# The last rows of an expert as a paired block, and smaller static shares

## The chip, the cores and the metric

The kernel runs on one core of a Trainium2 chip. The metric is the time of one execution on the device in microseconds (us), lower is better; the time given for a kernel is the median of its runs.

## What is computed

Three layers follow each other, in float32. Here is the reference, cut to the last one, which the change touches.

```python
def _moe2_ref(x, w_gate, w_output_gate, w1, w2):      # x: 1792 x 768, 8 experts, w1: 8 x 768 x 1024, w2: 8 x 1024 x 768
    logits = x @ w_gate
    e_idx = np.argmax(logits, axis=1)
    ...                                               # softmax: gate_w, one number per token
    eom = 1.0 / (1.0 + np.exp(-(x @ w_output_gate)))
    for e in range(E):
        mask = e_idx == e
        h = np.maximum(x[mask] @ w1[e], 0.0)
        ye = h @ w2[e]
        out[mask] = gate_w[mask, None] * eom[mask, e, None] * ye

def reference(**kwargs):
    attn_out = _attn_ref(...)                         # 4 batches, 12 heads, 448 tokens, 64 features
    x = attn_out.transpose(0, 2, 1, 3).reshape(1792, 768)
    x = _moe_ref(x=x, ...)                            # (sigmoid(x @ w_gate) * (x @ w_val)) @ w_out
    return _moe2_ref(x=x, ...)
```

Each token goes to one expert, the one of its largest logit.

## The kernel before

**Precision.** TensorE has a fast format, float32r, that keeps fewer bits of a number than float32. A float32 operand is therefore split into an upper part rounded to float32r and a lower part, the rest. A product of two split operands is taken in three passes: upper by upper, upper by lower, lower by upper. In the names `whi` and `wlo` are the parts of a weight piece (128 x 768), `gh` and `gl` those of the transposed tokens, `hh` and `hl` those of the hidden layer. In the trace both formats read as f32 matmuls.

**The stages.** Attention and the first dense layer come first and overlap; in them the rows of an expert's region in memory, `xg`, are filled with zeros in advance (`zero_rows`), and at their end a routing step gives every token a slot in its expert's region; scatters on GpSimd's queue put the tokens there. A planning step (`plan`) sorts the experts by count. The last part, `moe2`, then takes the experts in that order, j = 0 to 7, and for expert j a fixed number of rows, `CAPS[j]`, its static share. If an expert has more rows than its share, a branch at the end (`tc.If(some > 0)`, L1041 on) takes the remaining ones, 128 at a time, with the weights read again.

**One expert.** `gather(j)` reads its rows from `xg` by blocks of 128 (L918; the last block may be shorter) and, for a short block, copies of the row scales onto further partitions. `turn(j)` transposes them on TensorE (L936), ScalarE takes the upper part `gh` (L938) and VectorE the lower part `gl` (L939). `up2(j, f)`, for each of eight hidden blocks f, does 18 matmuls (six feature blocks by three passes, L957) with 128 x 128 of weights as the stationary operand and `CAPS[j]` columns of tokens as the moving one; ScalarE then takes relu and upper part (L963), VectorE the lower part (L964). `down2(j)` goes through the eight weight pieces of the second product; for each block of 128 rows the hidden block is the stationary operand and 384 columns of the weights the moving one, in two halves by three passes (L988), six matmuls. `finish(j)` multiplies by the row scale, on ScalarE (L1013) and in the last expert also VectorE (L1009), and scatters the rows to the output (L1016).

**The last rows.** A block of fewer than 128 rows has a path of its own (L980). The hidden rows stay whole in `hw`, float32 (L968), and so do the weights (`raw`); its 64 (or 32) rows take 64 (or 32) columns of the array, two (or four) such tiles side by side, each for a part of the 768 output columns:

```python
if rows < 128:
    c = DM * rows // 128
    for n in range(128 // rows):
        nc.tensor.matmul(
            ps[i, 0][n * rows:(n + 1) * rows, 0:c], lhsT=hw[f][:, 0:rows],
            rhs=w[2][:, LG + n * c:LG + (n + 1) * c], start=(f == 0), stop=(f == NF2 - 1))
```

**Weights and order.** An expert has 16 weight pieces of 384 KB. SyncE's queue loads them up to six ahead (L112), and they are split two ahead: ScalarE makes the upper part (L120), VectorE or GpSimd in turn the lower one (L122). The split parts stand in rings of four. The order of instructions on each engine is set by the framework's scheduler, which moves them within what the data allow; while `down2(j)` runs, the transposes of expert j + 1 are put between its matmuls, one feature block at a time, and parts of short blocks can come between the upward matmuls.

Of the kernel before, what the change touches and what calls it, by code (L numbers as in the profile page):

```python
# [8 lines left out]
F32 = mybir.dt.float32  # L9
# [10 lines left out]
CH = 112                       # queries or keys of a chunk; S is four of them  # L20
NPAIR = B * H // 2             # pairs of heads; a pair fills 128 features
# [5 lines left out]
LG = 2 * NE                    # logit columns beside the 768 of the output  # L27
WO = DM + LG
ROW = DM + 2                   # scale, token id, features
CAPS = [384, 320, 288, 256, 256, 256, 256, 192]   # rows that the static part takes, experts by count  # L30
CAPMAX = max(CAPS)
SQ_ACT = 1, 2                  # pairs whose squares ScalarE takes, and groups by their first pair whose roots VectorE
NEWTON_V = 0, 1
DIRECT = 0, 1, 2               # pairs whose rows of key scales come from the tensor engine alone
PARTS = 2                      # a piece of float64 comes in that many parts
# the last downward product of each half: blocks a to g, logits of its two token groups, their turn, the routing
FINAL = "a0b1ctrdefg", "01trabcdefg"
# what each slot of pair 0 prepares: splits, stats or key rows up to a pair, before all else where it is a capital
PREP = "s1 t2", "K1", "s2", "K2", "", "", "t4", ""
UNIT = 128.0                   # moe 1's outputs are kept divided by it: 1 / 256 comes with w_out, 2 with the gate  # L40
# [3 lines left out]
def attn_moe_moe_kernel(ctx, tc, qk, tokqk, tokv, g, wup, wout, wr, w1, w2, out):  # L44
# [26 lines left out]
    # ---------------------------------------------------------------- weights  # L71
    # a piece is 128 x 768, the 16 logit columns before it where it has them;
    # in: its float32 words are in SBUF, split: they lie there as two float32r parts
# [10 lines left out]
    def piece_in(n):  # L84
# [4 lines left out]
        if kind == "wide":  # L89
            for c in range(0, DM, DM // PARTS):  # L90
# [6 lines left out]
                # the upper word with its exponent in float32's place but for three bits, the lower one's upper three  # L97
# [67 lines left out]
    # -------------------------------------------------------------- attention  # L165
    # pools of which the first part of the attention has a second lot, in place of the moe's
# [54 lines left out]
    def halves(p):  # L221
        """the heads of a pair, by slices: the first pair's one by one"""
        return (slice(0, 1), slice(1, 2)) if p == 0 else (slice(0, 2),)
# [52 lines left out]
    def inv_root(grp):  # L276
        """(mean of squares + 1e-6) ** -0.5 by Newton's steps"""
# [20 lines left out]
    def row_bank():  # L298
        """a bank for what goes between the scores and the transposes, of its own as long as there is one"""
        if lots["ps_k"][2] is not None:  # L300
            return lots["ps_k"][2].tile([128, 4, CH], F32, tag="k", name="k")
        return tile_of("ps_t", [128, 4, CH], F32, "t")

    def krow(p):
# [4 lines left out]
        if p in DIRECT:  # L309
            # the first ones without the way through memory  # L310
# [159 lines left out]
    def prep(i):  # L470
        """what the first pairs need, in the slots of pair 0"""
# [25 lines left out]
    # -------------------------------------- logit columns: w_out times the router's weights  # L497
# [43 lines left out]
    # ------------------------------------------------------------------- moe 1  # L541
# [117 lines left out]
    # ----------------------------------------------------------------- routing  # L659
# [3 lines left out]
    def route(half):  # L663
# [23 lines left out]
        # ranks: tokens before this one of the same expert  # L687
# [9 lines left out]
        # the chosen expert's probability and output gate  # L697
# [4 lines left out]
        # slots  # L702
# [33 lines left out]
    def plan(tot):  # L736
        """Experts by falling count: tab = 8 experts, 8 counts past the static rows, 8 blocks of those, their sum."""
# [13 lines left out]
        # m[j, e] = (rank of e is j)  # L751
# [16 lines left out]
    # --------------------------------------------------------------- emission  # L768
# [15 lines left out]
    def setup2():  # L784
# [6 lines left out]
        # tri[t', t] = 1 where t' < t  # L791
# [39 lines left out]
    n = 0  # L831
# [34 lines left out]
    # second half: features come back and are split  # L866
# [15 lines left out]
def moe2(nc, tc, ctx, xg, w1, w2, out, tab, ident, add, ldpiece, drop, raw2, first):  # L882
# [31 lines left out]
    def gather(j):  # L914
        # float32's words as float32r, for transposes in one pass
        t = g_p.tile([128, 3, ROW], F32R, tag="g", name="g")
        for i, (r, n) in enumerate(blocks(j)):
            nc.sync.dma_start(out=t.bitcast(F32)[0:n, i, :], in_=xg[bass.ds(reg(j) * NT + r, n), :])  # L918
            for c in range(n, 128, n) if n < 128 else ():
                nc.sync.dma_start(out=t.bitcast(F32)[c:c + n, i, 0:1], in_=xg[bass.ds(reg(j) * NT + r, n), 0:1])  # L920
# [22 lines left out]
    def full(j):          # rows in blocks of 128  # L943
        return CAPS[j] // 128 * 128

    def up2(j, f):
# [13 lines left out]
        hh[f] = h_p.tile([128, CAPMAX], F32R, tag=f"hh{f}", name="hh")  # L960
        hl[f] = h_p.tile([128, CAPMAX], F32R, tag=f"hl{f}", name="hl")
        c0 = full(j)
        nc.scalar.activation(out=hh[f][:, 0:c0], in_=ps[:, 0:c0], func=ACTF.Relu)  # L963
        nc.vector.scalar_tensor_tensor(  # L964
            out=hl[f][:, 0:c0], in0=ps[:, 0:c0], scalar=0.0, in1=hh[f][:, 0:c0], op0=ALU.max, op1=ALU.subtract)
        if c0 < c:
            hw[f] = h_p.tile([128, 64], F32, tag=f"hw{f}", name="hw")
            nc.vector.tensor_scalar(out=hw[f][:, 0:c - c0], in0=ps[:, c0:c], scalar1=0.0, scalar2=None, op0=ALU.max)  # L968

    def down2(j):  # L970
        bl = blocks(j)
        ps = {(i, n): ps_d.tile([128, 512], F32, tag=f"d{i}{n}", name="d") for i in range(len(bl)) for n in range(2)}
        for f in range(NF2):
            w = ldpiece(("d", j, f))
            for i, (r, rows) in enumerate(bl):
                if rows < 128:
                    # few rows: column tiles of the array side by side, in float32
# [20 lines left out]
    def finish(j, ps):  # L998
        t = g_t.pop(j)
        for i, (r, rows) in enumerate(blocks(j)):  # L1000
            y = y_p.tile([128, DM], F32, tag="y", name="y")
            parts = 128 // rows if rows < 128 else 2
            c = DM // parts
            for n in range(parts):
                o, p = (i, n), 0
                if rows < 128:
                    o, p = (i, 0), n * rows
                if j == NE - 1 and n % 2:
                    nc.vector.tensor_scalar(  # L1009
                        out=y[0:rows, n * c:(n + 1) * c], in0=ps[o][p:p + rows, 0:c],  # L1010
                        scalar1=t.bitcast(F32)[p:p + rows, i, 0:1], scalar2=None, op0=ALU.mult)
# [152 lines left out]
```

## Time and profile before

| what | value |
|---|---|
| median of 3 runs | 1309.38 us |
| lowest and highest run | 1302.68 and 1311.21 us |
| profiled execution: its span, first to last instruction | 1302.4 us |
| TensorE's granted clock, mean over the span | 0.971 of full speed |

The profile is of one execution. The page gives its span and no other time of it, and it does not say which of the three runs it was, if any. A matmul's duration in the trace reaches past the start of the next one, since they are pipelined; what a stream of them costs is the time from one start to the next. Times within the profile are counted from the start of the span. The expert part begins at about 959 us.

### The profile page before, as it was taken

Reading aid. Unit: us, or ns where it says so; the run is one execution under the profiler, and the core shown is the slowest. Engines: PE = TensorE matmul, PEld = TensorE weight load, DVE = VectorE, ACT = ScalarE, POOL = GpSimd, SP = SyncE. Lnnn points to the kernel's source line nnn. Section 1 sums busy time; section 2 is a strip of 40 time slices with the busy share of each in tenths; the row PEclk is TensorE's granted clock in tenths of the full one; section 3 lists DMA queues with packets and bytes.
Section 4 is the critical chain, followed back from the end, with each engine's and each line's share of the span. In section 5 each row is a group of like instructions: output and inputs, shape, how many; then the busy total and the mean of one; then the engine's idle time right before and its main releaser. Section 6 shows DMA issues by size and latency. Waiting matters only on the chain.

```text
span 1302.4 us, 19952 instructions
## 1 busy us (share of the span) xinstructions
PE 1202.5 (92%) x7121; PEld 1041.0 (80%) x7121; DVE 737.0 (57%) x1688; ACT 593.4 (46%) x1173; POOL 387.0 (30%) x323
## 2 busy tenths in 40 slices
PE   4888889899899998998989999999969999999996
PEld 3656657678778887777879999999969888999994
DVE  7988987877678684855673143443443223333331
ACT  4666775556454553535332322212123344555552
POOL 3555655323142220411041000000032334444442
PEclk9897899999999999999999999999979999999999
DMA  9567557655436376595334111111074435665660
GB/s 218 141 160 181 160 148 216 180 162 167 123 125 196 107 218 181 148 237 145 123 130 155 54 49 61 50 56 42 1 278 165 168 103 183 251 223 209 208 218 19
DMA packets 79198, 194.04 MB, mean 149 GB/s; under 512 B 10543, under 2 KB 29487, under 8 KB 79088
## 3 DMA queue, kind: packets, MB, share of 16 engines
q1 hardware_dynamic: 76560, 181.64, 46.9%
q0 software_dynamic: 2528, 11.03, 2.2%
q8 instruction: 58, 0.95, 0.3%
q14 instruction: 52, 0.43, 0.1%
HBM read 154.97 MB, written 38.93 MB: 149 GB/s over the span
## 4 chain that ended last, share of the span: by engine, by line
PE 51%; DMA 3%; DVE 2%; issue 1%; SPq 1%; POOL 0%; ACT 0%; POOLq 0%; DVEq 0%
PE m L551 15%; PE d L988 11%; PE m L574 9%; PE u L957 8%; PE d L957 3%; DMA w<-in_wup_dram 2%; PE d L980 1%; PE a L430 1%; PE u L936 1%; DMA xg<-zrow 0%; DMA rs<-rsd 0%; DMA g<-xg 0%; PE t L409 0%; SPq L900 0%; PE m L593 0%
## 5 line engine op out<-in xcount | busy, mean ns | idle before, releaser
L120 ACT ACTIVATE whi<-raw 128x768 fp32r<-128x768 f32 (+1 forms) x200 | 167.0, 845 | 288.0 <-PE m L574 56.7
L122 POOL TENSOR_TENSOR wlo<-raw,whi 128x768 fp32r<-128x768 f32 (+1 forms) x100 | 190.8, 1913 | 312.8 <-ACT whi L120 289.1
L551 PE MATMUL m<-xh,whi 128*128 128x448 f32 x576 | 214.1, 372 | 6.6 <-DVE tanh L563 5.8
L122 DVE TENSOR_TENSOR wlo<-raw,whi 128x768 fp32r<-128x768 f32 (+1 forms) x100 | 101.3, 1017 | 205.9 <-ACT whi L120 197.6
L551 PE MATMUL m<-xl,whi 128*128 128x448 f32 x576 | 212.3, 369 | 0.0
L551 PE MATMUL m<-xh,wlo 128*128 128x448 f32 x576 | 210.5, 366 | 0.0
L381 ACT ACTIVATE e<-e,m,sy 112x448 f32<-112x448 f32 x192 | 144.9, 756 | 91.5 <-DVE m L378 90.8
L374 DVE CUSTOM_DVE_ANT_0 e<-s,rb 112x448 f32<-112x448 f32 x192 | 115.8, 612 | 19.4 <-PE s L363 11.5
L409 PE MATMUL t<-ident,e 112*112 112x112 f32 x768 | 112.4, 274 | 15.2 <-DVE et L415 5.3
L551 PEld LDWEIGHTS m<-xh,whi 128*128 128x128 f32 x576 | 109.2, 189 | 18.1 <-DVE tanh L563 6.5
L409 PEld LDWEIGHTS t<-ident,e 112*112 112x112 f32 x768 | 89.1, 140 | 43.1 <-issue 10.8
L574 PE MATMUL m<-whi,hhi 128*128 128x392 f32 (+1 forms) x336 | 115.5, 349 | 4.7 <-DVE acc L580 4.7
L551 PEld LDWEIGHTS m<-xl,whi 128*128 128x128 f32 x576 | 109.1, 189 | 9.6 <-issue 1.7
L574 PE MATMUL m<-wlo,hhi 128*128 128x392 f32 (+1 forms) x336 | 115.2, 343 | 1.3 <-POOL wlo L122 1.3
L551 PEld LDWEIGHTS m<-xh,wlo 128*128 128x128 f32 x576 | 109.0, 189 | 8.8
L430 PE MATMUL a<-et,v 112*64 112x224 f32 x768 | 110.9, 386 | 4.5 <-DVE xr L436 3.5
L362 PE MATMUL s<-K,Q 128*112 128x448 f32 x192 | 86.8, 452 | 30.5 <-DVE m L374 19.5
L574 PE MATMUL m<-whi,hlo 128*128 128x392 f32 (+1 forms) x336 | 114.2, 340 | 0.0
L335 POOL TENSOR_TENSOR Q<-qk,Q 64x896 fp32r<-64x896 f32 (+1 forms) x25 | 54.2, 2168 | 186.6 <-DVE Q L334 75.6
L417 ACT ACTIVATE et<-t 112x448 f32<-112x448 f32 x168 | 86.7, 531 | 29.2 <-PE t L409 28.9
L580 DVE TENSOR_TENSOR acc<-m,acc 128x392 f32<-128x392 f32 (+1 forms) x140 | 77.2, 559 | 33.6 <-PE m L574 32.4
L729 POOL DMA_INDIRECT xg<-acc,slot x14 | 14.4, 1029 | 272.5 <-DVE slot L706 268.6
(203 smaller groups left out, 2435.5 us busy)
## 6 DMA issues: line engine op xcount, KB each, us to landing
raw<-in_w_dram SPq DMA_DIRECT2D x128, 384.0 KB
qk<-in_qk_dram SPq DMA_DIRECT2D x46, 448.0 KB
w<-in_wup_dram SPq DMA_DIRECT2D x48, 384.0 KB
tok<-in_tokqk_dram SPq DMA_DIRECT2D x23, 448.0 KB
wf<-raw SPq DMA_DIRECT2D x24, 384.0 KB
w<-in_wout_dram SPq DMA_DIRECT2D x24, 384.0 KB
raw<-wf SPq DMA_DIRECT2D x24, 384.0 KB
rb<-rkd SPq DMA_DIRECT2D x21, 392.0 KB
```

Source lines behind the costliest of these rows:

```text
L120: nc.scalar.activation(out=hi[:, c:], in_=t[:, c:], func=ACTF.Copy)
L122: eng.tensor_tensor(out=lo[:, c:], in0=t[:, c:], in1=hi[:, c:], op=ALU.subtract)
L362: nc.tensor.matmul(ps, lhsT=lhs, rhs=K1_t[p][:, h, :], start=True, stop=False)
L374: nc.vector.tensor_tensor_reduce(out=e, in0=ps, in1=rb_t[p][:, h, :], scale=1.0, scalar=-3.0e38, op0=ALU.mult, op1=ALU.max, accum_out=m[:, ...
L381: nc.scalar.activation(out=e, in_=e, func=ACTF.Exp, scale=r_t[p][:, i:i + 1], bias=m[:, 1:2], accum_out=sum_t[p][:, i:i + 1])
L409: nc.tensor.transpose(ps[0:CH, kc, :], e[:, kc * CH:(kc + 1) * CH], ident[0:CH, 0:CH])
L417: nc.scalar.activation(out=dst, in_=ps[0:CH], func=ACTF.Copy)
L430: nc.tensor.matmul(ps[64 * h:64 * h + 64, hf * 2 * CH:(hf + 1) * 2 * CH], lhsT=v_t[p][:, h, kc, :], rhs=ets[h][:, kc, :], start=(kc == 0), ...
L551: nc.tensor.matmul(ps[:, 0:S], lhsT=a, rhs=x, start=(n == 0), stop=(n == 3 * KD - 1))
L574: nc.tensor.matmul(ps[:, 0:c1 - c0], lhsT=l, rhs=r, start=(i == 0), stop=(i == 5))
L957: nc.tensor.matmul(ps[:, 0:c], lhsT=a, rhs=x[:, k, 0:c], start=(n == 0), stop=(n == 3 * KD - 1))
L988: nc.tensor.matmul(ps[i, n][0:rows, 0:384], lhsT=l, rhs=s[:, c0:c0 + 384], start=(f == 0 and q == 0), stop=(f == NF2 - 1 and q == 2))
```

## The change

Two things are changed.

A last block of exactly 64 rows (`PAIRED`) is no longer computed in float32. Its upper parts and its lower parts are laid side by side in `hh`, 64 + 64 columns, as one stationary operand of 128 columns. Two passes, one with the upper and one with the lower part of the weights, then give the products of the upper rows on partitions 0 to 63 and of the lower rows on 64 to 127; `finish` adds the two halves: ScalarE scales the lower half into `y`, VectorE scales the upper half and adds. Such a block takes four matmuls a weight piece. A block of 32 rows keeps the old path, and blocks of over 64 rows take the ordinary path, where a block of 112 or 96 rows is now possible.

The static shares are smaller in four places: 384 to 320 (expert 0), 256 to 240, 224 and 192 (experts 4, 5 and 6). Experts 0, 1, 6 and 7 now end with a block of 64, expert 2 with one of 32. The rest of the difference is comments left out and line numbers moved by them; the first layers are the same.

```diff
-CAPS = [384, 320, 288, 256, 256, 256, 256, 192]   # rows that the static part takes, experts by count
+CAPS = [320, 320, 288, 256, 240, 224, 192, 192]
+PAIRED = 64
...
     def gather(j):
-            for c in range(n, 128, n) if n < 128 else ():
+            for c in range(n, 2 * n if n == PAIRED else 128, n) if n <= PAIRED else ():
...
-    def full(j):          # rows in blocks of 128
-        return CAPS[j] // 128 * 128
+    def full(j):
+        return sum(n for _, n in blocks(j) if n > PAIRED)
...
     def up2(j, f):
-        hh[f] = h_p.tile([128, CAPMAX], F32R, tag=f"hh{f}", name="hh")
+        hh[f] = h_p.tile([128, CAPMAX + PAIRED], F32R, tag=f"hh{f}", name="hh")
...
-        nc.scalar.activation(out=hh[f][:, 0:c0], in_=ps[:, 0:c0], func=ACTF.Relu)
+        c1 = c if c - c0 == PAIRED else c0
+        nc.scalar.activation(out=hh[f][:, 0:c1], in_=ps[:, 0:c1], func=ACTF.Relu)
...
-        if c0 < c:
-            hw[f] = h_p.tile([128, 64], F32, tag=f"hw{f}", name="hw")
+        if c0 < c1:
+            nc.vector.scalar_tensor_tensor(
+                out=hh[f][:, c1:c1 + PAIRED], in0=ps[:, c0:c1], scalar=0.0, in1=hh[f][:, c0:c1], op0=ALU.max,
+                op1=ALU.subtract)
+        elif c0 < c:
+            hw[f] = h_p.tile([128, PAIRED], F32, tag=f"hw{f}", name="hw")
...
     def down2(j):
-                if rows < 128:
+                if rows == PAIRED:
+                    for n in range(2):
+                        c0 = LG + n * 384
+                        for q in range(2):
+                            nc.tensor.matmul(
+                                ps[i, n][:, 0:384], lhsT=hh[f][:, r:r + 2 * rows], rhs=w[q][:, c0:c0 + 384],
+                                start=(f == 0 and q == 0), stop=(f == NF2 - 1 and q == 1))
+                    continue
+                if rows < PAIRED:
...
     def finish(j, ps):
-            parts = 128 // rows if rows < 128 else 2
+            parts = 128 // rows if rows < PAIRED else 2
             c = DM // parts
+            scale = t.bitcast(F32)[:, i, 0:1]
             for n in range(parts):
+                dst = y[0:rows, n * c:(n + 1) * c]
+                if rows == PAIRED:
+                    nc.scalar.activation(
+                        out=dst, in_=ps[i, n][rows:2 * rows, 0:c], func=ACTF.Copy, scale=scale[rows:2 * rows])
+                    nc.vector.scalar_tensor_tensor(
+                        out=dst, in0=ps[i, n][0:rows, 0:c], scalar=scale[0:rows], in1=dst, op0=ALU.mult, op1=ALU.add)
+                    continue
```

On TensorE, in expert 7's downward product, before: `hw` is the float32 block of 64 rows, with 64 of the array's columns.

```order
L988 MATMUL d<-whi,hh 128x384
L988 MATMUL d<-wlo,hh 128x384
L988 MATMUL d<-whi,hl 128x384
L980 MATMUL d<-raw,hw 64x384 x2
L988 MATMUL d<-whi,hh 128x384
L988 MATMUL d<-wlo,hh 128x384
L988 MATMUL d<-whi,hl 128x384
```

The same place after (L1003 is the ordinary block, L987 the paired one):

```order
L1003 MATMUL d<-whi,hh 128x384
L1003 MATMUL d<-wlo,hh 128x384
L1003 MATMUL d<-whi,hl 128x384
L987 MATMUL d<-whi,hh 128x384
L987 MATMUL d<-wlo,hh 128x384
L987 MATMUL d<-whi,hh 128x384
L987 MATMUL d<-wlo,hh 128x384
L1003 MATMUL d<-whi,hh 128x384
```

Two float32 matmuls on 64 columns have given way to four of the ordinary shape.

On TensorE, in the downward product of expert 5, where the transposes of expert 6 stand (`identr` marks a transpose, its shape ends with the rows turned), before:

```order
L936 MATMUL u<-identr,g 128x128 x2
L988 MATMUL d<-whi,hh 128x384
L988 MATMUL d<-wlo,hh 128x384
L988 MATMUL d<-whi,hl 128x384
L988 MATMUL d<-whi,hh 128x384
L988 MATMUL d<-wlo,hh 128x384
L988 MATMUL d<-whi,hl 128x384
```

The same place after; the 96 columns are the block of expert 5 with 96 rows:

```order
L1003 MATMUL d<-wlo,hh 128x384
L1003 MATMUL d<-whi,hl 128x384
L937 MATMUL u<-identr,g 128x128
L937 MATMUL u<-identr,g 128x64
L1003 MATMUL d<-whi,hh 96x384
L1003 MATMUL d<-wlo,hh 96x384
L1003 MATMUL d<-whi,hl 96x384
```

The second transpose of each feature block has 64 rows now instead of 128, and expert 5's second block has 96 columns as its stationary operand.

On VectorE, between expert 0 and expert 1, before (`gl` is the lower part of expert 1's transposed tokens, `hl` and `hw` belong to expert 1's first hidden block):

```order
L939 TENSOR_TENSOR gl<-u,gh 128x320 x2
L122 TENSOR_TENSOR wlo<-raw,whi 128x768
L939 TENSOR_TENSOR gl<-u,gh 128x320
L122 TENSOR_TENSOR wlo<-raw,whi 128x768
L964 SCALAR_TENSOR_TENSOR hl<-u,hh 128x256
L968 TENSOR_SCALAR hw<-u 128x64
```

The same place after (`y` are output rows of expert 0):

```order
L123 TENSOR_TENSOR wlo<-raw,whi 128x768
L940 TENSOR_TENSOR gl<-u,gh 128x320
L1025 SCALAR_TENSOR_TENSOR y<-d,g,y 64x384 x2
L123 TENSOR_TENSOR wlo<-raw,whi 128x768
L966 SCALAR_TENSOR_TENSOR hl<-u,hh 128x256
L969 SCALAR_TENSOR_TENSOR hh<-u,hh 128x64
```

The two additions into `y` stand ahead of a weight split and of the first hidden block; before, that split follows `gl` at once.

## Rows read from the trace of the kernel before

**Rows 1.** The page, busy time: us, share, instructions.

```profile
PE 1202.5 (92%) x7121; PEld 1041.0 (80%) x7121; DVE 737.0 (57%) x1688; ACT 593.4 (46%) x1173; POOL 387.0 (30%) x323
```

**Rows 2.** Windows, experts 0, 4, 6, 7, tail: us; busy (count) PE PEld DVE ACT POOL; clock; DMA; GB/s.

```profile
966.00:1022.00 56.00, 55.94 (x307) 54.55 (x307) 20.01 (x29) 23.83 (x42) 18.01 (x10) 0.95 0.51 173
...
1151.00:1186.00 35.00, 35.00 (x254) 34.79 (x254) 13.07 (x23) 19.21 (x35) 16.81 (x11) 1.00 0.63 226
...
1221.00:1257.00 36.00, 36.00 (x252) 34.66 (x251) 12.59 (x22) 18.73 (x35) 16.66 (x10) 1.00 0.66 225
1257.00:1292.00 35.00, 34.50 (x227) 26.20 (x225) 10.20 (x24) 14.09 (x25) 14.78 (x9) 1.00 0.24 81
1292.00:1303.00 11.00, 0.00 (x0) 0.00 (x0) 0.78 (x2) 0.23 (x1) 1.90 (x2) 0.70 0.15 51
```

**Rows 3.** Waits of TensorE's weight loads, 1116 to 1292: us, times, longest.

```profile
PEld d L988 <- POOL wlo L122: 0.6, 1, 0.6
```

**Rows 4.** Waits, 960 to 1303, ScalarE's split.

```profile
ACT whi L120 <- PE u L957: 48.2, 31, 5.2
```

**Rows 5.** The chain: start, us, what; upward 384, 320, 256, 192 columns, downward.

```profile
990.76 6.24 PE u L957 x36
...
1022.50 2.50 PE u L957 x17
...
1155.27 2.12 PE u L957 x18
...
1261.47 2.01 PE u L957 x18
```

```profile
1133.01 4.20 PE d L988 x24
```

**Rows 6.** The chain, first pieces of expert 7's downward product.

```profile
1273.54 1.07 PE d L988 x6
1274.61 0.80 PE d L980 x4
1275.40 1.24 PE d L988 x6
```

**Rows 7.** Timeline of TensorE at two turns, 128 + 64 rows and 128 + 128.

```profile
1242.13 0.40 PE L936 MATMUL u<-identr,g 128*128 128x128 f32 x2
...
1242.75 0.33 PE L988 MATMUL d<-wlo,hh 128*128 128x384 f32 x1
...
1207.08 0.29 PE L936 MATMUL u<-identr,g 128*128 128x128 f32 x2
...
1207.45 0.34 PE L988 MATMUL d<-wlo,hh 128*128 128x384 f32 x1
```

**Rows 8.** Timeline, the last transposes of expert 0.

```profile
965.22 1.01 PE L936 MATMUL d<-identr,g 128*128 128x128 f32 x6 [1.17 <-DMA g<-xg]
```

**Rows 9.** Windows, the first upward matmuls.

```profile
966.00:971.00 5.00, 4.94 (x16) 4.45 (x16) 4.24 (x7) 4.34 (x9) 1.98 (x2) 0.50 1.03 412
```

**Rows 10.** The chain at the end.

```profile
1290.61 0.56 PE d L988 x2
...
1292.27 0.63 DVE y L1009
...
1292.93 0.90 POOL out_dram L1016
...
1294.23 0.91 POOL out_dram L1016
```

**Rows 11.** Timelines, VectorE's split and TensorE's third upward group of expert 1.

```profile
1025.90 1.65 DVE L122 TENSOR_TENSOR wlo<-raw,whi 128x768 fp32r<-128x768 f32 x1 [4.77 <-ACT whi L120]
```

```profile
1028.16 0.38 PE L957 MATMUL u<-gh,whi 128*128 128x320 f32 x1 [0.40 <-DVE hw L968]
```

More of the change, by code (lines that the diff above doesn't have):

```diff
@@ L1001, in finish @@
             y = y_p.tile([128, DM], F32, tag="y", name="y")
-            parts = 128 // rows if rows < 128 else 2
+            parts = 128 // rows if rows < PAIRED else 2
             c = DM // parts
+            scale = t.bitcast(F32)[:, i, 0:1]
             for n in range(parts):
+                dst = y[0:rows, n * c:(n + 1) * c]
[5 more added lines that the diff above has]
+                    continue
                 o, p = (i, n), 0
-                if rows < 128:
+                if rows < PAIRED:
                     o, p = (i, 0), n * rows
@@ L1009, in finish @@
                     nc.vector.tensor_scalar(
-                        out=y[0:rows, n * c:(n + 1) * c], in0=ps[o][p:p + rows, 0:c],
-                        scalar1=t.bitcast(F32)[p:p + rows, i, 0:1], scalar2=None, op0=ALU.mult)
+                        out=dst, in0=ps[o][p:p + rows, 0:c], scalar1=scale[p:p + rows], scalar2=None, op0=ALU.mult)
                     continue
                 nc.scalar.activation(
-                    out=y[0:rows, n * c:(n + 1) * c], in_=ps[o][p:p + rows, 0:c], func=ACTF.Copy,
-                    scale=t.bitcast(F32)[p:p + rows, i, 0:1])
+                    out=dst, in_=ps[o][p:p + rows, 0:c], func=ACTF.Copy, scale=scale[p:p + rows])
             s = nc.gpsimd.indirect_dma_start(
```

## The prediction

> **What bounds the kernel now.** I read first the page's busy times and then a table of windows, one for each expert of the last part. TensorE is busy for 92% of the span [rows 1], and in the expert part for all of it: 35.00 of 35 us in expert 4, 36.00 of 36 in expert 6, while ScalarE, GpSimd and VectorE stand at 19, 17 and 13 us [rows 2]. The waits say the same from both sides. In the 176 us of experts 3 to 7 the weight loads of TensorE waited for a GpSimd split once, 0.6 us [rows 3]; ScalarE, which splits the weights, waited 48 us for TensorE to release them [rows 4]. So each matmul that goes from this part is worth its spacing, the time from its start to the next one's. The chain of waits gives that spacing, as time over count: going up, 6.24/36 = 0.173 us with 384 columns, 2.50/17 = 0.147 with 320, 2.12/18 = 0.118 with 256 and 2.01/18 = 0.112 with 192; going down 4.20/24 = 0.175 [rows 5].
>
> **The change part by part** (experts 0 to 7 in order of size; the routing of the reference on its inputs gives them 264, 262, 255, 254, 216, 211, 174 and 156 rows).
>
> *Expert 0, 384 to 320.* Upward 144 matmuls: 144 x (0.173 - 0.147) = 3.8 us. Downward the third block of 128 (six matmuls a piece) becomes a paired block of 64 (four), over eight pieces 16 fewer: 16 x 0.175 = 2.8. Together -6.6. Its first 5 us run at a granted clock of 0.50, the lower level, after the gather's idle time [rows 9]; that stays.
>
> *Experts 1 and 7, the last 64 rows.* Before, they go in full float32 with 64 columns of the array a time. Each such run takes 0.80 us, and the six ordinary matmuls between two runs take 1.24 instead of 6 x 0.175 = 1.05 [rows 6], so entering and leaving costs 0.19; a run is 1.0 us. Expert 7's downward stage lasts from 1273.54 [rows 6] to 1290.61 + 0.56 = 1291.17 [rows 10]: 17.6 us. Afterwards it holds 48 + 32 = 80 matmuls of one kind: 80 x 0.175 = 14.0, -3.6. Expert 1 has nine such runs in the order of before, 9.0 us, against 32 x 0.175 = 5.6: -3.4.
>
> The Trainium skill, TensorEngine Tiling (Array Packing), Key Properties, says that changing the tiling mode drains TensorE, and its table promises up to twofold speed for column tiles of 64. The trace agrees with the first by the 0.19 us; of the second it shows little, as the packed run of 0.80 is longer than the four full-width matmuls (0.70) that replace it.
>
> *Expert 6, 256 to 192.* Its second block turns into a paired one, 16 matmuls fewer: -2.8.
>
> *Narrower moving operands in experts 4, 5, 6 (240, 224, 192).* Below 256 columns the spacing hardly falls: 0.118 at 256 and 0.112 at 192 are the two ends for 240 and 224, so 144 matmuls save between 0 and 0.9 us each. From 384 columns down to 256 each 64 fewer bring about 0.027, the next 64 only 0.006, so I read 0.112 as a floor; 240 columns, 144 fewer than 384, would come to 0.173 - 144/64 x 0.027 = 0.112 and just reach it. 3 x 0.9 = -2.7.
>
> The Trainium skill, TensorE: Matmul & The Clock Gate, Back-to-back issue gap, puts the gap at columns/2.4 GHz + 2.5 ns, for 192 columns 82.5 ns. The trace does not agree (0.112); by that rule the three would save an estimated 6.7 us.
>
> *A transpose of 64 rows for expert 6.* It moves into expert 5's downward stage. A turn with 128 + 64 rows lasts from 1242.13 to 1242.75, one with 128 + 128 from 1207.08 to 1207.45 [rows 7]: 0.25 us more, six times: +1.5. The turns of 112 and 96 rows (experts 4 and 5) appear nowhere; their ends are 0 and +1.5 each, and I take 0, as they lie nearer to 128 than to 64.
>
> *Start.* The last transposes wait 1.17 us for the third gather [rows 8], which brings half the rows now, but another small DMA is queued behind it and six 64-row transposes follow: between -1.0 and +0.5, taken -0.5.
>
> *A new wait on VectorE.* The paired block is finished in two steps: ScalarE scales the lower half into y, then VectorE adds the upper half (a VectorE piece of y takes 0.63 us [rows 10]). VectorE stands in order: behind the two additions are the next expert's weight split and the release of its first upward bank. At that place before, a split of 1.65 us at 1025.90 already delays the release, and TensorE's third upward group begins only at 1028.16, with 0.40 us idle [rows 11]. Two additions cost some 1.3 us, but begin while VectorE was idle anyway. At the ends of experts 0, 1 and 6 I put 0 to 1 us each, +1.0 together. Elsewhere the added 64-column pieces on VectorE replace ones of the same size, or lie in its idle time (13 of 35 us busy [rows 2]); the smaller zero fill runs beside attention: 0.
>
> *Tail.* Before, the y pieces end with a VectorE one at 1292.27 + 0.63, then two scatters start at 1292.93 and 1294.23 [rows 10]. Now the last block needs two ScalarE and two VectorE steps in series with the first block's. The second scatter has 1.3 us of cover behind the first; the chain is some 1.2 longer: 0 to +1.2, taken +0.6.
>
> Sum: -6.6 - 3.6 - 3.4 - 2.8 - 2.7 + 1.5 - 0.5 + 1.0 + 0.6 = -16.5 us. Against the profiled execution's span of 1302.4 this is 1285.9. The median of the three runs is 7.0 above that span and the lowest run 0.3, so I set the difference against the median: 1309.4 - 16.5 = 1292.9, in round numbers 1293, -1.3%.
>
> **The rivals.** *The array changes its mode for 112 and 96 rows too.* For it speaks the 64-row turn [rows 7], against it only that these lie nearer to 128. It costs two sets of turns (+3.0) and, if the stationary operands of 112 and 96 columns drain it as well, 16 blocks x 0.19 = +3.0: 1299.
>
> *The weight split becomes the bound.* With TensorE some 2 to 4 us shorter in experts 4 to 7, ScalarE, GpSimd or the transfers would set the pace, and the terms of experts 4 to 7 (3.6 + 2.8 + 2.7 = 9.1) would be lost: 1302. Against it: expert 6 would take 36 - 2.8 - 0.9 = 32 us with ScalarE at 19 of it; expert 7's transfers have nearly ended when its downward stage begins, 81 GB/s in that window against 226 [rows 2].
>
> *The spacing goes on falling with the columns.* From 384 to 256 it falls by 0.055 for 128 columns, and at that slope 192 columns would give 0.090 and the three shares 144 x (0.007 + 0.014 + 0.028) = 7.0 instead of 2.7 us: 1289. Against it stands the row with 192 columns at 0.112 [rows 5]. The Trainium skill, TensorE: Matmul & The Clock Gate, Back-to-back issue gap, would have it so.
>
> *The other side: the branch for overflowing rows opens.* A share too small by a single row makes an expert run one more block of 128 after everything else, with all 16 weight pieces read again. At 226 GB/s [rows 2] a piece of 0.393 MB takes 1.74 us, 16 take 28, and the end of 11 us [rows 2] comes after that once more: +39, 1332. The counts decide: the lowered shares have 56, 24, 13 and 18 rows to spare, so only other inputs would open it.
>
> **How the numbers follow.** Forecast 0.74, its own range 1285 to 1299; mode changes 0.11; weight split 0.09; falling spacing 0.04; overflow 0.02. The three runs lie within 8.5 us, so I widen the range to 1283 to 1302: that leaves out the overflow, a little of the split's case and the tails of the first. A measurement of this kernel can tell about 1% from no change; the borders are 1296.3 and 1322.5. Faster by over 1%: most of the forecast (0.64), a third of the mode case (0.04), a fifth of the split's (0.02) and the falling spacing (0.04), 0.74. Slower by over 1%: the overflow and a rest, 0.02. Within: 0.24.
>
> **What would show it right or wrong.** Right: the paired blocks stand as runs of 0.175 us without a longer gap on either side; expert 7's downward stage takes some 14 us; expert 0 some 49 instead of 56; expert 6 some 32; upward spacings of 0.112 at 240 and 224 columns; expert 5 loses to 64-row turns what it gains. Wrong: gaps of 0.1 us and more around 96 or 112 rows; TensorE idle at the first upward groups of experts 1, 2 or 7 for more than 1 us each, behind VectorE's additions; waits of weight loads for ScalarE or GpSimd in experts 4 to 7; any instruction of the overflow loop; or a difference that arises before the expert part, where the order on TensorE is nearly unchanged.

## The result, and the profile after

The kernel after takes 1289.53 us (median of four runs, 1289.33 to 1292.87), against 1309.08 for the kernel before with a fourth run added to its three: a ratio of 0.9867, 95% interval 0.9834 to 0.9899. The forecast was 1293.0, 16.5 us below the median of the three runs; the time fell by 19.6. The profiled execution is the run of 1292.87 us, and its span is 1291.1; that of the kernel before was 1302.4.

The page of the kernel after, busy times as in [rows 1]:

```profile
PE 1187.7 (92%) x7089; PEld 1039.7 (81%) x7089; DVE 746.0 (58%) x1711; ACT 594.1 (46%) x1174; POOL 387.1 (30%) x323
```

TensorE is busy for the same 92% of a shorter span and has lost 14.8 us of work, with 32 instructions fewer.

Windows of the kernel after, with the columns of [rows 2]; each reaches from an expert's first upward matmul to the next one's, the last from the last matmul to the end:

```profile
973.83:1023.37 49.54, 48.44 (x291) 47.06 (x292) 20.06 (x37) 23.07 (x41) 17.99 (x10) 0.97 0.58 197
1023.37:1069.80 46.43, 46.43 (x292) 45.62 (x291) 15.45 (x32) 21.36 (x37) 18.46 (x12) 1.00 0.51 173
1069.80:1113.56 43.76, 43.44 (x318) 38.06 (x317) 15.78 (x32) 20.68 (x37) 18.02 (x12) 1.00 0.52 178
...
1148.45:1182.48 34.03, 34.03 (x253) 33.79 (x253) 13.10 (x23) 18.95 (x35) 16.79 (x11) 1.00 0.64 229
1182.48:1217.93 35.45, 35.45 (x253) 33.47 (x253) 12.81 (x23) 18.95 (x35) 17.01 (x11) 1.00 0.62 214
1217.93:1250.13 32.20, 32.20 (x236) 31.06 (x235) 12.45 (x30) 18.14 (x33) 16.40 (x10) 1.00 0.74 251
1250.13:1280.68 30.55, 30.55 (x227) 30.11 (x226) 11.22 (x27) 14.84 (x27) 14.84 (x9) 1.00 0.29 93
1280.68:1291.10 10.42, 0.00 (x1) 0.00 (x0) 1.44 (x3) 0.99 (x2) 1.91 (x2) 0.67 0.16 54
```

The same stretches of the kernel before, where their lengths differ most:

```profile
966.29:1022.34 56.05, 56.05 (x307) 54.84 (x308) 19.99 (x29) 23.88 (x42) 18.31 (x10) 0.95 0.50 171
1022.34:1072.50 50.16, 49.76 (x291) 41.40 (x290) 15.77 (x30) 20.73 (x37) 17.60 (x11) 1.00 0.47 160
...
1257.32:1291.50 34.18, 34.18 (x225) 25.88 (x224) 9.44 (x23) 13.27 (x24) 14.50 (x9) 1.00 0.24 79
```

TensorE is still busy all the time in experts 4 to 7. Expert 7 has nearly as many matmuls as before (227 and 225) and takes 3.6 us less, so what left is time per matmul. The lengths of the stages in us, here and in the experiments below (the expert part is the span from the first upward matmul on):

| kernel | 0 | 1 | 2 | 3 | 4 | 5 | 6 | 7 | tail | expert part |
|---|---|---|---|---|---|---|---|---|---|---|
| before | 56.05 | 50.16 | 43.35 | 34.97 | 34.99 | 35.06 | 36.45 | 34.18 | 10.90 | 336.1 |
| after | 49.54 | 46.43 | 43.76 | 34.89 | 34.03 | 35.45 | 32.20 | 30.55 | 10.42 | 317.3 |
| paired_only | 55.79 | 47.05 | 44.17 | 34.96 | 34.85 | 34.85 | 36.26 | 30.22 | 10.47 | 328.6 |
| shares_only | 52.66 | 48.34 | 43.38 | 35.09 | 34.07 | 35.48 | 34.98 | 34.74 | 11.02 | 329.8 |
| ordinary_64 | 52.14 | 49.66 | 44.44 | 35.01 | 34.05 | 35.41 | 35.32 | 32.92 | 10.14 | 329.1 |
| f32_one_tile | 57.12 | 54.10 | 44.50 | 34.92 | 34.04 | 35.42 | 39.96 | 37.58 | 9.68 | 347.3 |
| full_turn | 48.21 | 46.43 | 46.78 | 34.90 | 34.03 | 33.98 | 31.01 | 30.33 | 10.48 | 316.1 |
| full_turn_g3 | 48.19 | 46.36 | 43.61 | 35.14 | 34.12 | 34.04 | 31.07 | 30.46 | 10.52 | 313.5 |
| gather_3 | 49.44 | 46.36 | 43.61 | 35.14 | 34.12 | 35.46 | 32.29 | 30.67 | 10.42 | 317.5 |

The expert part is 18.8 us shorter; the span of this one pair is 11.3 shorter, since the first upward matmul stands at 973.83 here and at 966.29 before. That is why the table compares the expert part.

The chain of waits of the kernel after, in expert 7's downward product, where [rows 6] had float32 runs of 0.80 and ordinary groups of 1.24:

```profile
1266.76 1.07 PE d L1003 x6
1267.83 0.69 PE d L987 x4
1268.53 1.04 PE d L1003 x6
```

A paired run of four takes 0.69, and the six ordinary matmuls behind it 1.04, with no gap at the border. Upward groups of the same chain, with 320, 240, 224 and 192 columns, as [rows 5] had for other shares:

```profile
995.70 5.27 PE u L958 x36
...
1152.64 2.02 PE u L958 x18
...
1186.66 2.01 PE u L958 x18
...
1222.09 2.01 PE u L958 x18
```

That is 0.146 us a matmul at 320 columns, and 0.112 at 240, 224 and 192 alike.

### The profile page after: what moved, and what is told of

It is laid out like the page before. It is cut to its first block, busy times and chain, and to the rows that moved or that the text cites. A ratio compares the mean times of both kernels' runs of the same rounds, so it can differ in the third digit from the quotient of the medians.

```text
span 1291.1 us, 19932 instructions
## 1 busy us (share of the span) xinstructions
PE 1187.7 (92%) x7089; PEld 1039.7 (81%) x7089; DVE 746.0 (58%) x1711; ACT 594.1 (46%) x1174; POOL 387.1 (30%) x323
## 4 chain that ended last, share of the span: by engine, by line
PE 50%; DMA 2%; issue 1%; DVE 1%; ACT 0%; POOL 0%; SPq 0%; POOLq 0%; DVEq 0%
PE m L552 16%; PE d L1003 10%; PE m L575 9%; PE u L958 7%; PE d L958 3%; PE d L987 2%; PE u L937 1%; PE a L431 1%; PE t L410 0%; DMA raw<-in_w_dram 0%; DMA w<-in_wup_dram 0%; DMA xg<-acc,slot 0%; PE m L594 0%; PE d L995 0%; DVE xl L875 0%
## 5 line engine op out<-in xcount | busy, mean ns | idle before, releaser
L410 PEld LDWEIGHTS t<-ident,e 112*112 112x112 f32 x768 | 89.1, 141 | 44.2 <-issue 9.5
```

The lines of the kernel that those rows point to most:

```text
L410: nc.tensor.transpose(ps[0:CH, kc, :], e[:, kc * CH:(kc + 1) * CH], ident[0:CH, 0:CH])
```

## The experiments

Each is the kernel after with the edit shown (`...` stands for lines left out), and ratios are to the kernel before, timed on the same chip beside it.

**The paired blocks without the smaller shares** (paired_only).

```diff
-CAPS = [320, 320, 288, 256, 240, 224, 192, 192]
+CAPS = [384, 320, 288, 256, 256, 256, 256, 192]
```

> The paired block with the shares of before (384 320 288 256 256 256 256 192). Theory: each 64-row block gains its own 3.5 us whatever the shares are: expert 1 takes 46.4 us from its first upward matmul to expert 2's (50.2 before) and expert 7 about 30.5 (34.2 before), all other experts as before, so the expert part from its first upward matmul to the end of the span is 336.1 - 7.3 = 329 us and the time some 0.6% below before. Rival: most of the gain of the change comes from the smaller shares and the paired block is worth little by itself, since its two-step finish gives it back: expert part above 333 us.

Measured: 1305.01 us, ratio 0.9938 (0.991 to 0.9965), expert part 328.6. The window of expert 7:

```profile
1261.74:1291.97 30.23, 30.23 (x225) 29.91 (x224) 9.35 (x24) 14.07 (x25) 14.63 (x9) 1.00 0.29 89
```

Expert 7 loses 4.0 us and expert 1 loses 3.1, and the weight loads of expert 7 are busy for 29.91 us in place of 25.88: a float32 run leaves them little to do, a paired run keeps them going. In this kernel the first upward matmul stands at 973.8, and in the kernel before at 966.29, though TensorE and SyncE issue the same sequence up to 20 us ahead of it: single executions differ by some us in their first part, so the medians have to decide there.

**The smaller shares without the paired blocks** (shares_only): blocks of 64 rows go back to float32.

```diff
-        c1 = c if c - c0 == PAIRED else c0
+        c1 = c0
...
-                if rows == PAIRED:
+                if rows == -1:
...
-                if rows < PAIRED:
+                if rows <= PAIRED:
...
```

No block has -1 rows, so the paired path is never taken; `gather` and `finish` follow the same condition.

> The new shares with the 64-row block in float32 on column tiles, as before. Theory: against the changed kernel (expert part 317.3 us) experts 0, 1, 6 and 7 each lose some 3.5 us, 331 in all, so that the smaller shares alone are worth about 5 us and two of the four blocks exist only because of them. Rival: the smaller shares carry the gain, expert part below 323 us.

Measured: 1305.2 us, ratio 0.9921 (0.989 to 0.9953), expert part 329.8. Windows, experts 0 and 7:

```profile
973.84:1026.50 52.66, 52.66 (x290) 44.19 (x291) 19.84 (x37) 23.18 (x42) 18.21 (x10) 0.94 0.55 184
...
1257.84:1292.58 34.74, 34.74 (x228) 26.30 (x226) 10.07 (x23) 13.80 (x26) 14.80 (x9) 1.00 0.33 108
```

The shares alone bring 6.3 of the 18.8 us; in the four experts that end with 64 rows a float32 block costs 3.1, 1.9, 2.8 and 4.2 us more than a paired one. The two parts alone bring 6.3 and 7.5 us; the remaining 5.0 come only from both, for two of the four blocks of 64 rows are made by the new shares and made cheap by the pairing.

**The 64 rows on the ordinary three passes** (ordinary_64), with 64 columns of the array as the stationary operand.

```diff
-        return sum(n for _, n in blocks(j) if n > PAIRED)
+        return sum(n for _, n in blocks(j) if n >= PAIRED)
...
-        c1 = c if c - c0 == PAIRED else c0
+        c1 = c0
...
-                if rows == PAIRED:
+                if rows == -1:
...
```

> The new shares with the 64-row block in the ordinary three passes, its stationary operands 64 columns wide, same number format as its neighbours. If entering and leaving costs 0.19 us because the columns of the array are re-tiled (the prediction's reading), each of the blocks costs 8 x (6 x 0.175 + 0.19) = 9.9 us against 5.6 paired, in four experts +17 us against the changed kernel's expert part (317.3): 334. If it was the change of the number format that cost, the runs show no longer gap at their borders and the sum is 8 x 2 x 0.175 = 2.8 an expert, +11: 328.

Measured: 1302.59 us, ratio 0.9901 (0.9869 to 0.9933), expert part 329.1. The timeline of TensorE where the stationary operand goes from 128 to 64 columns and back:

```profile
1043.96 0.33 PE L1003 MATMUL d<-whi,hl 128*128 128x384 f32 x1
1044.13 0.33 PE L1003 MATMUL d<-wlo,hh 128*64 128x384 f32 x1
1044.31 0.34 PE L1003 MATMUL d<-whi,hl 128*64 128x384 f32 x1
...
1044.65 0.34 PE L1003 MATMUL d<-whi,hl 128*64 128x384 f32 x1
1044.83 0.31 PE L958 MATMUL u<-gh,whi 128*128 128x320 f32 x1
```

The starts stand 0.17 to 0.18 us apart at both borders. A stationary operand of 64 columns alone, then, drains nothing, and the gap around the float32 runs needs another cause. The kernel after is faster than this one by the third pass: 16 matmuls a block at 0.175 would be 2.8 us, and the four experts differ by 2.6, 3.2, 3.1 and 2.4.

**Float32 without the second tile** (f32_one_tile): the 64 rows in float32 again, but both halves of the output in columns 0 to 63 of the array, one after the other.

```diff
-        c1 = c if c - c0 == PAIRED else c0
+        c1 = c0
...
-                if rows == PAIRED:
+                if rows == -1:
...
+                if rows == PAIRED:
+                    for n in range(2):
+                        nc.tensor.matmul(
+                            ps[i, n][0:rows, 0:384], lhsT=hw[f][:, 0:rows],
+                            rhs=w[2][:, LG + n * 384:LG + (n + 1) * 384], start=(f == 0), stop=(f == NF2 - 1))
+                    continue
...
```

> The new shares; the 64-row block in float32, but its two halves one after the other on the same 64 columns, so that no tile stands at column 64. If entering and leaving a float32 run costs by the number format, the longer gaps at its borders stay (0.27 before it, 0.28 after it); if by the tile at column 64, they fall to 0.175. On both readings the run itself takes twice as long, some 1.6 us instead of 0.80, if the two tiles of before ran side by side.

Measured: 1323.89 us in one run, expert part 347.3. The chain in expert 1, and the timeline at one of its runs:

```profile
1040.15 1.43 PE d L993 x4
1041.59 2.83 PE u L958 x18
1044.42 1.44 PE d L993 x4
```

```profile
1044.11 0.31 PE L958 MATMUL u<-gh,wlo 128*128 128x320 f32 x1
1044.35 1.50 PE L993 MATMUL d<-raw,hw 128*64 128x384 f32 x4
1045.78 0.41 PE L958 MATMUL u<-gh,whi 128*128 128x320 f32 x1
```

A run takes 1.43 in place of the 0.80 of [rows 6], so two tiles side by side did work at the same time in the kernel before: the packing gave a factor of 1.8. The border is still there with one tile (0.24 from the last upward matmul into the float32 run, where such matmuls are 0.147 apart; the kernel before, with two tiles, has the same 0.24 there, from 1038.01 to 1038.25). Together with the run before this puts the border's cost on the float32 format; the trace can't show what TensorE does there.

**The 64-row transposes filled up** (full_turn): the gather brings 64 more rows, and a 64-row block is transposed with 128.

```diff
+            if n == PAIRED:
+                nc.sync.dma_start(out=t.bitcast(F32)[n:2 * n, i, 2:], in_=xg[bass.ds(reg(j) * NT + r + n, n), 2:])
...
+                if n == PAIRED:
+                    n = 128
...
-        for r in range(0, CAPMAX, 128):
-            n = min(128, CAPMAX - r)
+        for r in range(0, CAPMAX + PAIRED, 128):
+            n = 128
```

> The changed kernel, but the 64-row blocks are transposed with all 128 rows (64 more rows are gathered, their columns are not used), and the zero fill reaches 384 rows. Theory (64-row transposes cost 0.25 us each turn through a change of the array's mode): the turns inside experts 0, 5 and 6 lose six times 0.25 us each, -4.5 us in the expert part: 313. Rival (the 64-row transpose waits for its rows or its bank): no change, 317, or some us more by the added gathers at the start.

Measured: 1295.46 us, ratio 0.9841 (0.9797 to 0.9886), expert part 316.1. Experts 0, 5 and 6 lose 1.3, 1.5 and 1.2 us, 0.20 to 0.25 us for each of their six 64-row turns: the price of such a turn is confirmed by taking it away. But expert 2 takes 3.0 us longer, and the expert part misses the 313 of the theory. The chain passes there through a scatter of the output and then a weight load, for which TensorE waits twice, 1.30 and 0.41 us. Windows around these waits and right behind them:

```profile
1084.90:1087.90 3.00, 1.30 (x19) 0.40 (x17) 1.39 (x3) 1.11 (x2) 0.66 (x1) 1.00 1.00 373
1087.92:1091.42 3.50, 3.50 (x19) 3.50 (x16) 0.00 (x0) 0.00 (x0) 0.00 (x0) 0.51 1.02 411
```

After the waits the granted clock is at the lower of TensorE's two levels for 3.4 us, the only time in the nine profiles of the table that it falls between an expert part's first 6 us and its tail. Thirteen upward matmuls stand 0.240 us apart there instead of 0.132, so some 1.4 of the 3.0 us come from the clock and the rest from the waits themselves. The waits of SyncE's queue from 1040 to 1120:

```profile
SPq L919 <- DMA out_dram<-y,g: 16.3, 1, 16.3
```

A gather on SyncE's queue waits 16.3 us for the scatter of an earlier expert, since it reuses the tile from which that scatter takes its scales and indices, and the weight loads queued behind it wait with it.

**Three gather tiles** (full_turn_g3, and gather_3 without the filled-up turns). In full_turn_g3 the lines of full_turn stay, but expert 0 keeps its shorter gather; gather_3 has the first of these edits alone.

```diff
-    g_p = pools.enter_context(tc.tile_pool(name="g", bufs=2))
+    g_p = pools.enter_context(tc.tile_pool(name="g", bufs=3))
...
+            if n == PAIRED and j > 0:
...
+                if n == PAIRED and j > 0:
```

> The transposes over all 128 rows for experts 1, 6 and 7 (not for expert 0, whose extra gather stood in the way at the start) and a third buffer for the gathered rows. Theory: expert 2 lost 3.0 us in the run before because the gather for expert 3 waits for the scatter of expert 1 (two buffers), and the weight loads stand behind it in SyncE's queue; with a third buffer expert 2 returns to 43.4 us, experts 5 and 6 stay at 34.0 and 31.0, and the expert part is 313, 1.3% of it below the changed kernel's 317.3. Rival: the weights are late because the added gathers take the transfers' time; expert 2 stays above 45.

> The changed kernel with a third buffer for the gathered rows alone. Theory: SyncE's wait of 16 us for the scatter goes, expert 2 loses its 0.3 us of idle TensorE (43.4 instead of 43.8 us), nothing else changes. Rival: unchanged 43.8.

Measured: full_turn_g3 1289.25 us, ratio 0.983 (0.9803 to 0.9857), expert part 313.5; gather_3 1296.83 in one run, expert part 317.5. Window of full_turn_g3, expert 2, and SyncE's wait at that place in gather_3:

```profile
1064.91:1108.52 43.61, 43.61 (x317) 38.22 (x317) 15.70 (x32) 20.76 (x37) 18.23 (x12) 1.00 0.46 142
```

```profile
SPq L919 <- PE u L937: 0.2, 1, 0.2
```

Expert 2 is back at 43.61 and TensorE is never idle in it, though experts 1, 6 and 7 keep their added gathers; that speaks for the queue and against the rival. What expert 0's added gather, left out here, had to do with it is not separated. The kernel after has the same wait of 16.3 us on SyncE, but its loads are nearly early enough: in the four profiles with its expert part (three of the kernel after, and zero_384 below) TensorE idles there for 0.1 to 0.7 us, waiting for a weight load, and with the third tile alone not at all. Expert 2 takes 43.5 to 44.2 us in those four, so the 0.15 us that gather_3 saves against the first of them is less than they differ.

**The branch for overflowing rows** (overflow): expert 3's share set 14 rows under its count of 254.

```diff
-CAPS = [320, 320, 288, 256, 240, 224, 192, 192]
+CAPS = [320, 320, 288, 240, 240, 224, 192, 192]
```

> The share of expert 3 lowered from 256 to 240, 14 rows below its 254, so that the branch for overflowing rows runs once. The prediction's price for one block is +39 us; saved by the narrower share 0.9. Expected 1289.5 - 0.9 + 39 = 1328. Rival: the branch reads its weights three at a time and computes in float32 without splits, each step waiting for the one before, and costs 60 us or more.

Measured: 1358.09 us in one run, expert part 384.1, 66.8 more than the kernel after. The branch's window, and the first rows of its timeline on TensorE:

```profile
1290.00:1356.00 66.00, 28.04 (x134) 19.26 (x134) 4.94 (x33) 3.38 (x10) 1.97 (x2) 0.73 0.36 110
```

```profile
1299.75 0.69 PE L1101 MATMUL ops<-ident,og 128*128 128x128 f32 x2 [21.09 <-DMA og<-xg]
```

For 14 rows TensorE waits 21 us before it starts, is busy for 28 of 66 us at a mean granted clock of 0.73, and the transfers move 110 GB/s: the branch is a chain of waits, as the rival had it, and not a stream of weights.

**The kernel after again, twice, beside two partners** (after_again, full_turn_g3_again; after_third, zero_384). zero_384 puts back the zero fill of 384 rows an expert (1.58 MB more on the page).

> The changed kernel once more, on the chip of the next run and for its first part: the order of its instructions before the expert part is that of the first profile. Theory: the expert part is 317.3 us again within 0.3; what lies before it (973.8 us in the first profile) differs by several us from one execution to the next, and with it the times.

> The version with 128-row transposes and a third gather buffer beside the changed kernel on one chip: expert part 313.5 again, 3.8 below, median 0.3% below the changed kernel's; the runs may be too far apart to show that much.

> The changed kernel, with the zeros of the sorted table once more written for 384 rows behind the last expert, as in the kernel before, and nothing else. The expert part is untouched and should be 317.3 us again (316.5 to 318.5). Theory A (the shorter zero fill and what it moves make the first part shorter by some 4 us, the difference of the medians left over when the expert parts are taken off): median near 1293.5 us, some 4 us above the run of the changed kernel beside it, and a first upward matmul that much later. Rival (the first part only varies from run to run, and the medians differed by chance): the two medians agree within 1.5 us.

> The changed kernel once more, as the partner of the run with the longer zero fill: median 1289.6 us (1288 to 1291.5), expert part 317.3 us, by either theory.

| kernel | median us | range | ratio to before |
|---|---|---|---|
| after_again | 1289.71 | 1288.67 to 1292.85 | 0.9832 (0.9807 to 0.9858) |
| full_turn_g3_again | 1288.28 | 1283.68 to 1291.58 | 0.9813 (0.9787 to 0.9839) |
| after_third | 1291.31 | 1282.94 to 1294.14 | 0.9827 (0.9797 to 0.9857) |
| zero_384 | 1294.95 | 1291.68 to 1298.22 | 0.9863 (0.9838 to 0.9888) |

The expert parts of after_again and after_third are 317.4 and 317.1 us, as expected, and that of full_turn_g3_again is 313.5. So full_turn_g3 is 3.8 and 3.9 us shorter in the expert part, and 1.4 us in the median, which can't be told from nothing. It also fills 384 rows with zeros. The run with the longer fill alone is 3.6 us above its partner, near the 4 expected of theory A, and four of its five times lie above all fifteen that were taken of the kernel after; its expert part is 317.7 us (1296.3 less 978.56). So the medians are for theory A. The other kernels with four runs or more agree: the median less the profile's expert part is 974.8 to 979.4 us for the five with the long fill (full_turn_g3 twice, paired_only, zero_384, full_turn) and 972.2 to 975.4 for the five with the short one (the kernel after three times, ordinary_64, shares_only), 3.2 us apart on the average, and wherever both kinds were timed on one chip, each with the long fill, the kernel before among them, lies above each with the short one. The profiles don't show where it happens. The zero writes of zero_384 and after_third (durations of one issue, then first and last start):

```profile
L811 SPq DMA_DIRECT2D xg<-zrow x24: 332/528/1290, 489.0 to 608.2; - x24
```

```profile
L811 SPq DMA_DIRECT2D xg<-zrow x24: 332/533/875, 484.7 to 602.2; - x24
```

The two executions stand 4.3 us apart before the first zero is written, and their fills last 119.2 and 117.5 us. Over all fourteen profiles the first zero write comes anywhere from 479.5 (before) to 489.3 (full_turn). By which wait the fill costs its some 3 us stays open.

## Why the prediction was right, and where it was not

By stages, the forecast's terms beside what the profile of the kernel after shows:

| term | predicted | measured |
|---|---|---|
| expert 0 | -6.6 | -6.5 |
| start, from the first transpose to the first upward matmul | -0.5 | -0.4 to -1.2 in three profiles |
| expert 1 | -3.4 | -3.7 |
| experts 2 and 3 | 0 | +0.4, -0.1 |
| expert 4 | -0.9 | -1.0 |
| expert 5, its 64-row turns and narrower operand | +0.6 | +0.4 |
| expert 6, second block and narrower operand | -3.7 | -4.3 |
| expert 7 | -3.6 | -3.6 |
| additions on VectorE at the boundaries | +1.0 | 0 |
| tail | +0.6 | -0.5 |

*TensorE bounds the expert part, and each matmul is worth its spacing: right.* The terms worked out so come within 0.6 us each, and the two halves of the change, run apart, come to 328.6 and 329.8.

*The floor of 0.112 us: right.* It holds at 240, 224 and 192 columns. At 240 the falling slope would have given nearly the same, 0.111 (0.118 less 0.007); 224, for which it would have given 0.104, refutes that rival. The Trainium skill (TensorE: Matmul & The Clock Gate, Back-to-back issue gap) gives the formula that the prediction took from it for an isolated matmul, and says that in a stream of weight loads and matmuls both set the spacing; so these rows, which are such a stream, do not test the formula, and no run here shows which of the two sets the 0.112.

*No mode change for 112 and 96 rows: right.* The timeline of the kernel after at turns with 112 rows (first two) and with 96:

```profile
1137.02 0.28 PE L937 MATMUL u<-identr,g 128*128 128x128 f32 x2
...
1137.39 0.33 PE L1003 MATMUL d<-wlo,hh 128*128 128x384 f32 x1
...
1168.76 0.27 PE L937 MATMUL u<-identr,g 128*128 128x128 f32 x2
...
1169.12 0.34 PE L1003 MATMUL d<-wlo,hh 128*128 128x384 f32 x1
```

From the first transpose to the second ordinary matmul they take 0.37 and 0.36 us, like the 0.37 of 128 + 128 rows in [rows 7]. Nor do the narrower stationary operands cost at their borders: in the downward products of experts 4 and 5 the starts from 128 to 112 or 96 columns and back are 0.17 to 0.18 us apart. The weight split never became the bound either: from 1113 to 1281 us the longest wait of a weight load on what the profile names was 0.3 us.

*The reading of the gaps around the float32 runs: the step that failed.* The price was right (0.80 + 0.19 us a run), but the prediction took the trace to agree that the change of the array's tiling drains it, and it took the packing to bring little. ordinary_64 has the same 64-column operands and no gap; f32_one_tile has one tile and the gap. What a float32 run pays at its borders it pays among float32r matmuls because of its format, and the packed tiles had nearly halved its length. The sum took no harm, since it used the price as measured; the part of the first rival that charged 16 blocks with 0.19 us at 112 and 96 columns did rest on the wrong cause. The rule of the Trainium skill on a drain (TensorEngine Tiling (Array Packing), Key Properties) may still stand behind the 0.25 us of a 64-row transpose, which full_turn took away; the runs show its price, not its cause.

*The additions on VectorE: mis-sized, 0 for +1.0.* They do what the prediction says, between expert 0 and 1 and with a wait for ScalarE before each:

```profile
1024.09 0.61 DVE L1025 SCALAR_TENSOR_TENSOR y<-d,g,y 64x384 f32<-64x384 f32 x1 [1.76 <-ACT y L1023]
1025.56 0.61 DVE L1025 SCALAR_TENSOR_TENSOR y<-d,g,y 64x384 f32<-64x384 f32 x1 [0.86 <-ACT y L1023]
1026.93 0.96 DVE L123 TENSOR_TENSOR wlo<-raw,whi 128x768 fp32r<-128x768 f32 x1 [0.76 <-ACT whi L121]
```

But the chain has TensorE's first 108 upward matmuls of expert 1 in one piece:

```profile
1023.53 15.81 PE u L958 x108
```

The stall of 0.40 us in [rows 11] is gone, though VectorE's split starts 3.56 us after the first upward matmul in both (1025.90 less 1022.34 and 1026.93 less 1023.37): it takes 0.96 us now instead of 1.65. GpSimd's own weight split of that moment, in the kernel before and after:

```profile
1024.86 1.86 POOL L122 TENSOR_TENSOR wlo<-raw,whi 128x768 fp32r<-128x768 f32 x1
1025.01 1.84 POOL L123 TENSOR_TENSOR wlo<-raw,whi 128x768 fp32r<-128x768 f32 x1
```

Before, it overlapped VectorE's split for 0.82 us; after, it ended at 1026.85, ahead of it. The expert parts of both profiles have 101 VectorE splits that no GpSimd split overlaps, and each takes 0.96 or 0.97 us. So the additions cost nothing here partly by luck: they lie where VectorE would have waited for ScalarE, and GpSimd's split moved out of the way, which the prediction did not foresee.

*The tail: mis-sized, and of the other sign.* The last two matmuls are the paired block's now, so ScalarE begins on the ordinary block 0.66 us before they end (0.31 before the change), and GpSimd issues the first scatter 1.09 us after the last matmul; before it was 1.43 (1292.93 in [rows 10] less 1291.50). The last rows of the timeline of the kernel after:

```profile
1281.24 1.13 DVE L1025 SCALAR_TENSOR_TENSOR y<-d,g,y 64x384 f32<-64x384 f32 x2 [0.25 <-ACT y L1023]
1281.77 0.99 POOL L1037 DMA_INDIRECT out_dram<-y,g  x1 [5.52 <-ACT y L1023]
1283.07 0.91 POOL L1037 DMA_INDIRECT out_dram<-y,g  x1 [0.30 <-issue]
```

VectorE's additions end at 1282.37, ahead of the second scatter at 1283.07: the cover of 1.3 us that the prediction names was enough, for the scatter of the 64 rows comes second.

*The overflow rival: mis-sized, 39 for 67 us.* It counted the weights' bytes and one more end, and left out the serial waits, 21 us of them in front of the first matmul.

*The first part: costed at 0 (the smaller zero fill), and open in its cause.* The expert part's -18.8 is 2.8 us more than the -16.0 of the terms that lie in it, most of that from the boundaries and the tail. But the medians fell by 19.6 in the first comparison, 23.3 and 20.7 in the later two. The medians favour a gain of some 3 to 4 us from the shorter fill; its place wasn't found.

## What to carry to other kernels

When a split float32 product has a block of half height left over, upper and lower parts side by side fill the stationary operand and cost two passes in place of three; here that was 2.4 to 3.2 us of an expert's time against the three passes and 1.9 to 4.2 against packed float32. Price a matmul by the time between starts in a stream of its own kind, and check before narrowing a moving operand whether the spacing has reached its floor. A shorter stage on the bounding engine brings what it promises only while the queues behind it keep up, so look for loads that stand behind a waiting transfer: here 1.7 us of waits made an expert 3.0 longer, as the clock fell behind them.

## What was not expected of the hardware

- The price at the border of float32 and float32r matmuls (0.19 us a run) goes with the format; 64 columns of the array beside 128 cost nothing in float32r.
- Two float32 tiles of 64 columns did run side by side: 0.80 us against 1.43 in one tile for the same products.
- A weight split on VectorE takes 0.96 us alone and 1.65 us with 0.82 us of GpSimd's split beside it.
- The start of expert 0 at the lower of TensorE's two clock levels (a granted clock of 0.50) lasts differently from run to run. In the profile of the kernel after it is over earlier than in that of after_third, and yet expert 0 lasts 49.54 us in both, since in the former TensorE then waits 1.10 us for ScalarE to empty a bank, at 982.08, and in the latter 0.31. Windows of 2.5 us of the kernel after, and of after_third:

```profile
973.83:976.33 2.50, 2.50 (x8) 2.26 (x9) 2.46 (x6) 2.50 (x7) 0.04 (x1) 0.50 0.99 380
976.33:978.83 2.50, 2.50 (x16) 2.50 (x16) 1.93 (x1) 1.58 (x3) 2.50 (x2) 0.85 1.02 404
```

```profile
971.81:974.31 2.50, 2.50 (x8) 2.26 (x9) 2.46 (x6) 2.50 (x7) 0.04 (x1) 0.50 1.01 396
974.31:976.81 2.50, 2.50 (x11) 2.50 (x11) 1.92 (x1) 1.28 (x2) 2.50 (x2) 0.50 1.03 412
```
